# x as one row spread by TensorE, ScalarE's row sums as a register loop, GpSimd as a loop of eight units

## The chip, the cores and the metric

One Trainium2 chip, one core. The metric is the device time of one execution in microseconds (us); lower is better. A verdict of faster or slower needs a difference of 2%. An execution over 1.5% above the fastest of its kernel is called slow, a single one unknown, any other fast.

## The reference, cut to what matters

Two independent attention blocks, A and B, each decode one token for a batch of 2, with 32 heads, a cache of 8192 positions and a head width of 192. Each has its own x, caches and weights:

```python
q = (x @ wq)                                   # x: (2, 1, 640)
scores = einsum("bhqd,bhkd->bhqk", q, k_cache) * 192 ** -0.5
p = softmax(scores)
o = einsum("bhqk,bhkd->bhqd", p, v_cache)
out = o.reshape(2, 1, 32 * 192) @ wo           # then A and B side by side
```

Every K and V is read once: 2 blocks x 2 batches x 32 heads = 128 units, each with 3 MB of K and 3 MB of V. With the weights that is 836.77 MB from HBM, the chip's main memory.

## The kernel before

Each unit multiplies its K by the query, broadcast to all partitions. VectorE forms the products of all 64 rows and sums 48 of them by halving; the other 16 rows ScalarE sums with one activation each. GpSimd finds the maximum over partitions, ScalarE takes the exponential, TensorE multiplies by V. SyncE issues all loads; K and V have two buffers each.

```python
def sp_x(blk, b):                              # x, one batch: 640 elements to [128, 5]
    src = blocks[blk]["x"][b, 0, :].rearrange("(c j) -> j c", j=128)
    ...
            return eng.dma_start(xT[blk][b][:], src).then_inc(xsem[blk], 16)

def xbc_copy(blk, b):                          # spread over 128 columns, for TensorE's weights
    return lambda eng: eng.tensor_copy(xbc[blk][b][:], xT[blk][b][:].unsqueeze(2).broadcast_to([128, DC, 128]))

def act_acc(u, t):                             # ScalarE: the sum of one row
    return lambda eng: eng.activation(prodA[u % 2][:, t, :], prodA[u % 2][:, t, :], ACTF.Identity,
                                      accum_out=sc[u % 2][:, t:t + 1])
...
for t in range(na_of(u)):                      # 16 rows, written out
    w = [("d1a", u), key("d3", u - 2), key("exp", u - 2)] if t == 0 else []
    put(act_tab, u, 10 + t, act_acc(u, t), w, ("acc", u) if t == na_of(u) - 1 else None)
...
# SyncE's order at the start: x of A (2 loads), wq, K0 (2 parts), wq, x of B (2 loads), K1, V0, ...
# K(u) waits until VectorE has read K(u-2); V(u) waits until TensorE has read V(u-2)
...
S_sp.emit(eng)          # every instruction written out
S_pool.emit(eng)        # every instruction written out
S_dve.emit(eng, 8)      # steady middle as a hardware loop with a body of 8 units
S_act.emit(eng, 8)
S_pe.emit(eng, 4)
```

`emit(eng, period)` finds the longest stretch of the program that repeats after `period` units and puts it into a register loop, then searches what lies before and after it in the same way. What is left, as at the two ends and the seam of blocks A and B, stays written out.

Of the kernel before, what the change touches and what calls it, by code (L numbers as in the profile page):

```python
# [6 lines left out]
ACTF = mybir.ActivationFunctionType  # L7
AXL = mybir.AxisListType
BF16 = mybir.dt.bfloat16
# [93 lines left out]
def build_kernel(nc, blocks, out, cfg=None):  # L103
    cfg = dict(cfg or {})
    NBLK = len(blocks)
    B, Hn, Sk, Dh = blocks[0]["k"].shape
    D = blocks[0]["x"].shape[2]
    assert B == 2 and Dh == 192 and Sk % 256 == 0 and D % 128 == 0
    T = Sk // 128
    DC = D // 128  # L110
# [4 lines left out]
    scale = float(Dh) ** -0.5  # L115

    NA_MAIN = min(cfg.get("NA", 16), T - 2)
    LAG = cfg.get("LAG", 2)
    LATE = LAG - 1
    NPB = 4  # L120
# [14 lines left out]
    def na_of(u):  # L135
        return NA_MAIN

# [10 lines left out]
    with ExitStack() as es:  # L148
        sb = lambda name, shape, dt, align=32: es.enter_context(nc.sbuf_tensor(name, shape, dt, align_bytes=align))
# [10 lines left out]
        prodA = [sb(f"prodA{i}", [128, NA_MAX, Dh], BF16) for i in range(2)]  # L160
        prodD = sb("prodD", [128, ND_MAX, Dh], BF16)
        sc = [sb(f"sc{i}", [128, T], F32) for i in range(2)]
# [3 lines left out]
        pb = [sb(f"pb{i}", [128, T // 2, 33], BF16) for i in range(NPB)]  # L166
        rs = [sb(f"rs{i}", [128, 1], F32) for i in range(2)]
        qbc = [sb(f"qbc{i}", [128, 2, Dh], BF16) for i in range(4)]
        xT = [[sb(f"xT{k}_{b}", [128, DC], BF16) for b in range(B)] for k in range(NBLK)]
        xbc = [[sb(f"xbc{k}_{b}", [128, DC, 128], BF16) for b in range(B)] for k in range(NBLK)]  # L170
        o_sb = sb("o_sb", [33, 2, 2, Dh], F32)
        ones33 = sb("ones33", [33, 1], F32)
# [5 lines left out]
        actd = sb("actd", [128, 2], F32)  # L178
# [6 lines left out]
        reg = {}  # L185
# [16 lines left out]
        def key(name, *idx):  # L202
            for i in idx:
                if i < 0:
                    return None
            return (name,) + tuple(idx)
# [27 lines left out]
        reg[("wq0b",)] = (wq0sem, 16)  # L234
        WQSPLIT = HG >= 4
        for k in range(NBLK):
            reg[("x", k)] = (xsem[k], 16 * B)
            reg[("odone", k)] = (osem[k], 32)

        def dma(out_ap, in_ap, s):  # L240
            return lambda eng: eng.dma_start(out_ap, in_ap).then_inc(s, 16)  # L241

        def sp_x(blk, b):
            src = blocks[blk]["x"][b, 0, :].rearrange("(c j) -> j c", j=128)

            def fn(eng):
                with nc.allow_non_contiguous_dma(reason="tiny x transpose load"):
                    return eng.dma_start(xT[blk][b][:], src).then_inc(xsem[blk], 16)  # L248
            return fn

        def sp_wq(w, part=None):
            blk = (w * HG) // Hn
# [35 lines left out]
                return dma(v_tile(u)[:], src, vsem[u % NV])  # L288
            return dma(v_tile(u)[:, t0:t1, :], src[:, t0:t1, :], sm)

        def xbc_copy(blk, b):
            return lambda eng: eng.tensor_copy(xbc[blk][b][:], xT[blk][b][:].unsqueeze(2).broadcast_to([128, DC, 128]))

        def pool_ar(u):
            return lambda eng: eng.partition_all_reduce(mg[u % 2][:], mp[u % 2][:], 128, bass.bass_isa.ReduceOp.max)  # L295
# [30 lines left out]
            s0 = 64 * (g % 2)  # L326
            return lambda eng: eng.reciprocal(rcT[(g // 2) % 2][s0:s0 + 64, :], lall[g % 2][s0:s0 + 64, :])

        def act_acc(u, t):
            return lambda eng: eng.activation(prodA[u % 2][:, t, :], prodA[u % 2][:, t, :], ACTF.Identity,  # L330
                                              accum_out=sc[u % 2][:, t:t + 1])

        def act_nb(u):
            return lambda eng: eng.activation(nb[u % 2][:], mg[u % 2][:], ACTF.Identity, scale=-scale)  # L334
# [45 lines left out]
        def pe_p0(qg):  # L380
            pr, b = qg // 2, qg % 2
            g0 = 2 * pr
            blk = g0 // Hn
            w = g0 // HG
            npr = HG // 2

            def at(slot, off):
                def fn(eng):
                    for c in range(DC):
                        ins = eng.matmul(qps[:, 0:QW], xbc[blk][b][:, c, :],  # L390
                                         wqs[:, slot, c, off].rearrange("p a n -> p (a n)") if slot is not w % 2 else
                                         wqs[:, slot, c, off],
                                         start=(c == 0), stop=(c == DC - 1))
                    return ins
                return fn
            fn = at(w % 2, slice((pr % npr) * QW, (pr % npr + 1) * QW))
            fn.same = (blk, b)
            fn.turn = lambda it: at(bass.ds((it + pr) // npr % 2, 1), bass.ds((it + pr) % npr * QW, QW))
            return fn, [("wq", w) if w == 0 else None, ("wq0b",) if (w == 0 and WQSPLIT and pr % npr >= 1) else None,
                        ("xbc", blk), key("a0", qg - 1)]  # L400

        def pe_pv(u, j0, j1):
            b = u % B
# [58 lines left out]
        def put(tab, slot, order, fn, waits, sig):  # L462
            tab[slot].append((order, len(tab[slot]), fn, waits, sig))

        for u in range(NU):
            g = u // B
            put(dve_tab, u + 1, 0, dve_d3(u), [("acc", u), ("r", u), key("ar", u - 2)], ("d3", u))
            put(dve_tab, u, 2, dve_d1a(u), [("k", u), ("a0", qg_of(u)), key("acc", u - 2)], ("d1a", u))
            put(dve_tab, u, 3, dve_d1b(u), [("k", u), ("kb", u) if u in KSPLIT else None, ("a0", qg_of(u)),
                                            key("r", u - 1)], ("d1b", u))  # L470
            put(dve_tab, u, 4, dve_lvl(u, 96), [("d1b", u)], ("l1", u))
            put(dve_tab, u, 5, dve_lvl(u, 48), [("l1", u)], ("l2", u))
            put(dve_tab, u, 6, dve_lvl(u, 24), [("l2", u)], ("l3", u))
            put(dve_tab, u, 7, dve_r(u), [("l3", u), key("d3", u - 2), key("exp", u - 2)], ("r", u))
            put(pool_tab, u + 1, 0, pool_ar(u), [("d3", u), key("nb", u - 2)], ("ar", u))
            put(pool_tab, u + 1, 1, pool_ls(u), [("exp", u), key("f2", g - 2)], ("ls", u))
            put(act_tab, u + 1, 0, act_nb(u), [("ar", u), key("exp", u - 2)], ("nb", u))
            put(act_tab, u + 1, 1, act_exp(u), [("nb", u), ("acc", u), ("r", u), key("pv", u - NPB)], ("exp", u))
            for t in range(na_of(u)):
                w = [("d1a", u), key("d3", u - 2), key("exp", u - 2)] if t == 0 else []  # L480
                put(act_tab, u, 10 + t, act_acc(u, t), w, ("acc", u) if t == na_of(u) - 1 else None)
            pc = pieces(u)
            w0 = [("exp", u), key("f1", g - 2), ("init",)]
            if pc is None:
                put(pe_tab, u + LATE, 0, pe_pv(u, 0, T // 2), w0 + [("v", u)], ("pv", u))
            else:
                for i, (t0, t1, sm) in enumerate(pc):
                    put(pe_tab, u + LATE, 0.1 * i, pe_pv(u, t0 // 2, t1 // 2), (w0 if i == 0 else []) + [("vp", u, i)],
                        ("pv", u) if i == len(pc) - 1 else None)
# [59 lines left out]
                    S_sp.add(sp_v(u, t0, t1, sm), waits=w)  # L549

        UG = HG * B
        for b in range(B):
            S_sp.add(sp_x(0, b))
        S_sp.add(sp_wq(0, 0) if WQSPLIT else sp_wq(0))
        korder = []
        nv = 0
# [8 lines left out]
        for kind, u in korder:  # L565
            if kind == "k":
                if u in KSPLIT:
                    S_sp.add(sp_k(u, 0), waits=[key("d1b", u - NK)])
                    S_sp.add(sp_k(u, 1))
                else:  # L570
                    S_sp.add(sp_k(u), waits=[key("d1b", u - NK)])
                if u == 0:
                    if WQSPLIT:
                        S_sp.add(sp_wq(0, 1))
                    for blk in range(1, NBLK):
                        for b in range(B):
                            S_sp.add(sp_x(blk, b))
                w = u // UG
                if u % UG == (4 if UG >= 8 else 1):
                    S_sp.add(sp_wo(w), waits=[key("f5", (w - 1) * HG // 2)])  # L580
                if u % UG == (3 if UG >= 8 else 0) and w + 1 < NWG:
                    S_sp.add(sp_wq(w + 1), waits=[key("pq", w * HG)])
            else:
                add_v(u)
# [4 lines left out]
            S_pool.add((lambda i: (lambda eng: eng.memset(pb[i][:], 0.0)))(i))  # L589
        S_pool.add(lambda eng: eng.memset(oTz[:], 0.0))  # L590
        S_pool.add(lambda eng: eng.memset(oTzL[:], 0.0), sig=("init",))
        for blk in range(1, NBLK):
            for b in range(B):
                S_pool.add(xbc_copy(blk, b), waits=[("x", blk)], sig=("xbc", blk) if b == B - 1 else None)
        for b in range(B):
            S_dve.add(xbc_copy(0, b), waits=[("x", 0)], sig=("xbc", 0) if b == B - 1 else None)
        S_act.add(lambda eng: eng.memzero(actd[:, 0:1]), sig=("actd",))
        S_act.add(lambda eng: eng.activation(actd[:, 1:2], actd[:, 0:1], ACTF.Exp), waits=[("actd",)])

        for tab, S in ((dve_tab, S_dve), (act_tab, S_act), (pe_tab, S_pe), (pool_tab, S_pool)):  # L600
            for slot in range(NSLOT):
# [4 lines left out]
        with nc.Block() as block:  # L606
            @block.sync
            def _(eng):
                S_sp.emit(eng)

            @block.gpsimd
            def _(eng):
                S_pool.emit(eng)

            @block.vector
            def _(eng):
                S_dve.emit(eng, 8)

            @block.scalar
            def _(eng):  # L620
                S_act.emit(eng, 8)

            @block.tensor
            def _(eng):
                S_pe.emit(eng, 4)
# [49 lines left out]
```

## Time and profile before

| | before |
|---|---|
| time in us: first three runs, median | 1959.01 (1957.16 to 1959.31) |
| profiled execution | 1957.15, span 1955.3 |
| HBM read | 836.77 MB, 428 GB/s over the span |
| DMA busy | 9 tenths or more in each of 40 slices |
| VectorE, TensorE, ScalarE, GpSimd busy | 85%, 57%, 46%, 8% |

The page of the kernel before, cut to the span, the DMA packets, the two queues that fetch instructions (the engines' programs, piece by piece as they run), and two groups (busy us, mean ns of one, then the idle time before them):

```profile
span 1955.3 us, 18519 instructions
...
DMA packets 56618, 837.10 MB, mean 428 GB/s; under 512 B 7432, under 2 KB 18320, under 8 KB 24208
...
q8 instruction: 11, 0.18, 0.0%
q14 instruction: 15, 0.12, 0.0%
...
L330 ACT ACTIVATE prodA<-prodA 128x192 bf16<-128x192 bf16 x2048 | 709.3, 350 | 125.3 <-DVE prodA L308 124.8
...
L315 DVE TENSOR_REDUCE mp<-sc 128x1 f32<-128x64 f32 x128 | 28.2, 220 | 13.8 <-issue 4.9
```

The kernel is bound by the DMA engines. The maximum over scores (L315), which needs ScalarE's sums as well as VectorE's, waits 13.8 us in the whole run, so ScalarE isn't late. The instruction fetches stand at 0.0% of the engines' time.

SyncE's issues in the timeline of the kernel before (start, length, what):

```profile
0.72 0.98 SPq L248 DMA_DIRECT2D xT<-in_A_x_dram  x2
1.75 0.52 SPq L241 DMA_DIRECT2D wqs<-in_A_wq_dram  x1
2.31 1.00 SPq L241 DMA_DIRECT2D kb<-in_A_k_cache_dram  x2
3.35 0.43 SPq L241 DMA_DIRECT2D wqs<-in_A_wq_dram  x1
3.83 7.38 SPq L248 DMA_DIRECT2D xT<-in_B_x_dram  x2
...
11.25 0.54 SPq L241 DMA_DIRECT2D kb<-in_A_k_cache_dram  x1
11.83 2.26 SPq L241 DMA_DIRECT2D vb<-in_A_v_cache_dram  x1
```

The first large load goes out behind two x loads. Two more hold SyncE for 7.4 us ahead of K1.

### The profile page before, as it was taken

How to read it: one execution, taken by the hardware profiler on the slowest of the kernel's cores; microseconds unless marked ns; L12 is line 12 of the kernel's file. 1: busy time of each engine (PE TensorE's matmuls, PEld its weight loads, DVE VectorE, ACT ScalarE, POOL GpSimd, SP SyncE). 2: the span in 40 equal slices, each digit the busy share in tenths (PEclk: the TensorE clock that was granted, in tenths of full speed). 3: DMA queues.
4: the chain of work that ended last, by engine and by line, in shares of the span. 5: the costliest groups of instructions: out<-in, count | busy, mean ns of one | idle time of the engine just before them, and what ended most of it. 6: DMA issues, size and time to landing. Idle time of an engine off the chain costs nothing.

```text
span 1955.3 us, 18519 instructions
## 1 busy us (share of the span) xinstructions
PE 1110.9 (57%) x5004; PEld 588.5 (30%) x5004; DVE 1656.2 (85%) x962; ACT 903.2 (46%) x4743; POOL 165.8 (8%) x270
## 2 busy tenths in 40 slices
PE   3455655656556564565556655556555556655567
PEld 1222332323223232332223332233332333323234
DVE  7799888888988889887988889888798788888886
ACT  4445454444544445444454445444454454444543
POOL 4103000000000000000000000000000000000000
PEclk7777777777777777777777767777677777777778
DMA  9999999999999999999999999999999999999998
GB/s 385 430 433 428 433 431 432 433 430 432 431 432 432 431 434 430 432 433 429 432 430 433 431 430 433 431 431 434 429 433 430 432 433 432 431 429 435 432 433 338
DMA packets 56618, 837.10 MB, mean 428 GB/s; under 512 B 7432, under 2 KB 18320, under 8 KB 24208
## 3 DMA queue, kind: packets, MB, share of 16 engines
q1 hardware_dynamic: 56576, 836.79, 99.9%
q8 instruction: 11, 0.18, 0.0%
q14 instruction: 15, 0.12, 0.0%
q10 hardware_dynamic: 16, 0.01, 0.0%
HBM read 836.77 MB, written 0.01 MB: 428 GB/s over the span
## 4 chain that ended last, share of the span: by engine, by line
DMA 74%; PE 23%; DVE 2%; issue 0%; SPq 0%; ACT 0%; DVEq 0%
DMA vb<-in_B_v_cache_dram 37%; DMA vb<-in_A_v_cache_dram 33%; PE ops L408 23%; DMA kb<-in_A_k_cache_dram 4%; DVE prodD L312 2%; DVE prodD L319 1%; DVE prodA L308 0%; DVE sc L323 0%; SPq L241 0%; PE oTps L428 0%; PE outps L444 0%; SPq L248 0%; DVE mp L315 0%; ACT out_sb L372 0%; ACT o_sb L353 0%
## 5 line engine op out<-in xcount | busy, mean ns | idle before, releaser
L408 PE MATMUL ops<-vb,pb 128*33 128x384 bf16 x4064 | 944.9, 407 | 830.7 <-DMA vb<-in_A_v_cache_dram 443.1
L408 PEld LDWEIGHTS ops<-vb,pb 128*33 128x33 bf16 x4064 | 476.1, 120 | 1297.9 <-issue 578.2
L330 ACT ACTIVATE prodA<-prodA 128x192 bf16<-128x192 bf16 x2048 | 709.3, 350 | 125.3 <-DVE prodA L308 124.8
L312 DVE TENSOR_TENSOR prodD<-kb,qbc 128x9216 bf16<-128x9216 bf16 x128 | 633.7, 4951 | 3.7 <-DMA kb<-in_A_k_cache_dram 3.7
L319 DVE TENSOR_TENSOR prodD<-prodD 128x4608 bf16<-128x4608 bf16 (+2 forms) x384 | 599.0, 1560 | 13.3
L308 DVE TENSOR_TENSOR prodA<-kb,qbc 128x3072 bf16<-128x3072 bf16 x128 | 225.2, 1759 | 243.1 <-DMA kb<-in_B_k_cache_dram 127.6
L330 ACT ACTIVATION_READ_ACCUMULATOR prodA<-prodA 128x1 f32 x2048 | 387.9, 189 | 0.0
L334 ACT ACTIVATE nb<-mg 128x1 f32<-128x1 f32 x128 | 26.0, 203 | 725.8 <-POOL mg L295 725.8
L295 POOL PARTITION_ALL_REDUCE mg<-mp x128 | 53.7, 419 | 1652.6 <-DVE mp L315 1652.6
L323 DVE TENSOR_REDUCE sc<-prodD 128x48 f32<-128x1152 bf16 x128 | 173.2, 1353 | 4.4
L299 POOL PARTITION_ALL_REDUCE lall<-rs x128 | 101.3, 791 | 111.1 <-ACT pb L337 111.1
L344 ACT ACTIVATE o_sb<-ops 1x384 f32<-1x384 f32 x63 | 30.1, 478 | 125.7 <-PE oTps L417 112.5
L417 PE MATMUL oTps<-ones,o_sb 33*128 33x1 f32 x372 | 69.8, 311 | 1.4 <-ACT o_sb L345 1.4
L417 PEld LDWEIGHTS oTps<-ones,o_sb 33*128 33x128 f32 x372 | 67.2, 258 | 11.3 <-issue 7.9
L390 PE MATMUL qps<-wqs,xbc 128*128 (+1 forms) x320 | 65.1, 335 | 6.8 <-DMA wqs<-in_A_wq_dram 6.0
L337 ACT ACTIVATE pb<-sc,nb 128x64 bf16<-128x64 f32 x128 | 52.2, 408 | 13.0
L368 ACT ACTIVATE qbc<-qps 128x384 bf16<-128x384 f32 x64 | 31.4, 491 | 45.1 <-PE qps L390 45.0
L315 DVE TENSOR_REDUCE mp<-sc 128x1 f32<-128x64 f32 x128 | 28.2, 220 | 13.8 <-issue 4.9
L390 PEld LDWEIGHTS qps<-wqs,xbc 128*128 128x128 bf16 x320 | 26.4, 99 | 31.2 <-issue 10.5
L345 ACT ACTIVATE o_sb<-ops 1x384 f32<-1x384 f32 x63 | 30.4, 482 | 0.7
L444 PE MATMUL outps<-wos,oTz 128*4 (+1 forms) x186 | 30.3, 299 | 0.5 <-ACT oTz L362 0.5
L337 ACT ACTIVATION_READ_ACCUMULATOR pb<-sc,nb 128x1 f32 x128 | 23.9, 186 | 0.0
(27 smaller groups left out, 68.4 us busy)
## 6 DMA issues: line engine op xcount, KB each, us to landing
vb<-in_A_v_cache_dram SPq DMA_DIRECT2D x64, 3072.0 KB, 22.2
kb<-in_B_k_cache_dram SPq DMA_DIRECT2D x64, 3072.0 KB, 22.4
kb<-in_A_k_cache_dram SPq DMA_DIRECT2D x63, 3072.0 KB, 22.4
vb<-in_B_v_cache_dram SPq DMA_DIRECT2D x61, 3072.0 KB, 22.1
wos<-in_A_wo_dram SPq DMA_DIRECT2D x8, 960.0 KB, 26.8
wqs<-in_B_wq_dram SPq DMA_DIRECT2D x8, 960.0 KB, 24.5
wos<-in_B_wo_dram SPq DMA_DIRECT2D x8, 960.0 KB, 26.8
wqs<-in_A_wq_dram SPq DMA_DIRECT2D x7, 960.0 KB, 24.5
```

The source lines that it names most:

```text
L295: return lambda eng: eng.partition_all_reduce(mg[u % 2][:], mp[u % 2][:], 128, bass.bass_isa.ReduceOp.max)
L299: return lambda eng: eng.partition_all_reduce(lall[g % 2][:, b:b + 1], rs[u % 2][:], 128, bass.bass_isa.ReduceOp.add)
L308: return lambda eng: eng.tensor_tensor(prodA[u % 2][:, 0:na, :], kb[u % NK][:, 0:na, :], qb_bc(u, na), ALU.mult)
L312: return lambda eng: eng.tensor_tensor(prodD[:, 0:T - na, :], kb[u % NK][:, na:T, :], qb_bc(u, T - na), ALU.mult)
L319: return lambda eng: eng.tensor_tensor(prodD[:, 0:nd, 0:w], prodD[:, 0:nd, 0:w], prodD[:, 0:nd, w:2 * w], ALU.add)
L323: return lambda eng: eng.tensor_reduce(sc[u % 2][:, na:T], prodD[:, 0:T - na, 0:24], AXL.X, ALU.add)
L330: return lambda eng: eng.activation(prodA[u % 2][:, t, :], prodA[u % 2][:, t, :], ACTF.Identity, accum_out=sc[u % 2][:, t:t + 1])
L337: return lambda eng: eng.activation(pb[u % NPB][:, :, ::32], sc[u % 2][:].rearrange("p (j a) -> p j a", a=2), ACTF.Exp, bias=nb[u % 2][:], ...
L368: return lambda eng: eng.activation(qbc[qg % 4][:], qps[:, 0:QW].rearrange("p (a d) -> p a d", a=2), ACTF.Identity)
L390: ins = eng.matmul(qps[:, 0:QW], xbc[blk][b][:, c, :], wqs[:, slot, c, off].rearrange("p a n -> p (a n)") if slot is not w % 2 else wqs[:, ...
L408: ins = eng.matmul(ops[(u // B) % 2][0:33, b, 0:QW], pb[u % NPB][:, j, :], vv[:, j, :], start=(j == 0), stop=(j == T // 2 - 1))
L417: ins = eng.matmul(oTps[:, 2 * i + b:2 * i + b + 1], o_sb[:, b, :, :].rearrange("p s (r i) -> p i (s r)", i=3)[:, i, :], ones33[:], start= ...
```

## The change

Its intent: take 2560 two-byte packets and their issue time off SyncE at the start; write ScalarE's 16 row sums as a register loop, five turns of three and one left over; give GpSimd's stream the loop that the others have. Cut to its core:

```diff
+        xrow = [sb(f"xrow{k}", [1, B, DC, 128], BF16) for k in range(NBLK)]
+        one1 = sb("one1", [1, 128], BF16)
...
-        def sp_x(blk, b):                      # 4 loads on SyncE, element by element
+        def ld_x(blk):                         # 2 loads on ScalarE's queue, x as one row
+            src = blocks[blk]["x"].rearrange("b o (c j) -> o b c j", j=128)
+            return dma(xrow[blk][:], src, xsem[blk])
...
-        def xbc_copy(blk, b): ...
+        def pe_x(blk, b):                      # TensorE spreads the row: row chunk x ones
+            def fn(eng):
+                for c in range(DC):
+                    ins = eng.matmul(xps(b)[:, c, :], xrow[blk][0:1, b, c, :], one1[:], start=True, stop=True)
+                return ins
+            return fn
+        # then PSUM to xbc: VectorE for A's batch 0, ScalarE for the other three
...
-        def act_acc(u, t): ...
+        def act_acc(u):
+            na = na_of(u); nl = (na - 1) // ROWS * ROWS          # ROWS = 3
+            def fn(eng):
+                ...
+                with eng.Fori(0, nl - ROWS + 1, ROWS) as i:
+                    for k in range(ROWS):
+                        one(pa[:, bass.ds(i + k, 1), :], s[:, bass.ds(i + k, 1)])
+                for t in range(nl, na):
+                    ins = one(pa[:, t, :], s[:, t:t + 1])
+                return ins
...
-                S_pool.emit(eng)
+                S_pool.emit(eng, 8)
```

More of the change, by code (lines that the diff above doesn't have):

```diff
@@ L117, in build_kernel @@
     NA_MAIN = min(cfg.get("NA", 16), T - 2)
+    ROWS = 3
     LAG = cfg.get("LAG", 2)
@@ L168, in build_kernel @@
         qbc = [sb(f"qbc{i}", [128, 2, Dh], BF16) for i in range(4)]
-        xT = [[sb(f"xT{k}_{b}", [128, DC], BF16) for b in range(B)] for k in range(NBLK)]
+        xrow = [sb(f"xrow{k}", [1, B, DC, 128], BF16) for k in range(NBLK)]
+        one1 = sb("one1", [1, 128], BF16)
         xbc = [[sb(f"xbc{k}_{b}", [128, DC, 128], BF16) for b in range(B)] for k in range(NBLK)]
@@ L236, in build_kernel @@
         for k in range(NBLK):
-            reg[("x", k)] = (xsem[k], 16 * B)
+            reg[("x", k)] = (xsem[k], 16)
             reg[("odone", k)] = (osem[k], 32)
@@ L241, in dma @@
             return lambda eng: eng.dma_start(out_ap, in_ap).then_inc(s, 16)
-        def sp_x(blk, b):
-            src = blocks[blk]["x"][b, 0, :].rearrange("(c j) -> j c", j=128)
-            def fn(eng):
-                with nc.allow_non_contiguous_dma(reason="tiny x transpose load"):
-                    return eng.dma_start(xT[blk][b][:], src).then_inc(xsem[blk], 16)
-            return fn
+        def ld_x(blk):
+            src = blocks[blk]["x"].rearrange("b o (c j) -> o b c j", j=128)
+            return dma(xrow[blk][:], src, xsem[blk])
         def sp_wq(w, part=None):
@@ L289, in sp_v, with xps, act_x, dve_x @@
             return dma(v_tile(u)[:, t0:t1, :], src[:, t0:t1, :], sm)
-        def xbc_copy(blk, b):
-            return lambda eng: eng.tensor_copy(xbc[blk][b][:], xT[blk][b][:].unsqueeze(2).broadcast_to([128, DC, 128]))
+        def xps(b):
+            return ops[b][:].rearrange("p a n -> p (a n)")[:, 0:D].rearrange("p (c m) -> p c m", m=128)
+        def pe_x(blk, b):
[4 more added lines that the diff above has]
+            return fn
+        def act_x(blk, b):
+            return lambda eng: eng.activation(xbc[blk][b][:], xps(b), ACTF.Identity)
+        def dve_x(blk, b):
+            return lambda eng: eng.tensor_copy(xbc[blk][b][:], xps(b))
         def pool_ar(u):
@@ L327, in dve_f2, with one @@
             return lambda eng: eng.reciprocal(rcT[(g // 2) % 2][s0:s0 + 64, :], lall[g % 2][s0:s0 + 64, :])
-        def act_acc(u, t):
-            return lambda eng: eng.activation(prodA[u % 2][:, t, :], prodA[u % 2][:, t, :], ACTF.Identity,
-                                              accum_out=sc[u % 2][:, t:t + 1])
+        def act_acc(u):
+            na = na_of(u)
+            nl = (na - 1) // ROWS * ROWS
+            def fn(eng):
+                pa, s = prodA[u % 2], sc[u % 2]
+                def one(row, col):
+                    return eng.activation(row, row, ACTF.Identity, accum_out=col)
+                with eng.Fori(0, nl - ROWS + 1, ROWS) as i:
[4 more added lines that the diff above has]
+                return ins
+            return fn
         def act_nb(u):
@@ L399, in pe_p0 @@
             return fn, [("wq", w) if w == 0 else None, ("wq0b",) if (w == 0 and WQSPLIT and pr % npr >= 1) else None,
-                        ("xbc", blk), key("a0", qg - 1)]
+                        ("xbc", blk, b), key("a0", qg - 1)]
         def pe_pv(u, j0, j1):
@@ L478, in build_kernel @@
             put(act_tab, u + 1, 1, act_exp(u), [("nb", u), ("acc", u), ("r", u), key("pv", u - NPB)], ("exp", u))
-            for t in range(na_of(u)):
-                w = [("d1a", u), key("d3", u - 2), key("exp", u - 2)] if t == 0 else []
-                put(act_tab, u, 10 + t, act_acc(u, t), w, ("acc", u) if t == na_of(u) - 1 else None)
+            put(act_tab, u, 10, act_acc(u), [("d1a", u), key("d3", u - 2), key("exp", u - 2)], ("acc", u))
             pc = pieces(u)
@@ L551, in build_kernel @@
         UG = HG * B
-        for b in range(B):
-            S_sp.add(sp_x(0, b))
         S_sp.add(sp_wq(0, 0) if WQSPLIT else sp_wq(0))
@@ L574, in build_kernel @@
                         S_sp.add(sp_wq(0, 1))
-                    for blk in range(1, NBLK):
-                        for b in range(B):
-                            S_sp.add(sp_x(blk, b))
                 w = u // UG
@@ L591, in build_kernel @@
         S_pool.add(lambda eng: eng.memset(oTzL[:], 0.0), sig=("init",))
+        S_dve.add(lambda eng: eng.memset(one1[:], 1.0), sig=("one1",))
+        for blk in range(NBLK):
+            S_act.add(ld_x(blk))
+        for b in range(B):
+            S_pe.add(pe_x(0, b), waits=[("x", 0), ("one1",)], sig=("xp", 0, b))
+        S_dve.add(dve_x(0, 0), waits=[("xp", 0, 0)], sig=("xbc", 0, 0))
+        S_act.add(lambda eng: eng.memzero(actd[:, 0:1]), sig=("actd",))
+        S_act.add(lambda eng: eng.activation(actd[:, 1:2], actd[:, 0:1], ACTF.Exp), waits=[("actd",)])
+        S_act.add(act_x(0, 1), waits=[("xp", 0, 1)], sig=("xbc", 0, 1))
         for blk in range(1, NBLK):
             for b in range(B):
-                S_pool.add(xbc_copy(blk, b), waits=[("x", blk)], sig=("xbc", blk) if b == B - 1 else None)
-        for b in range(B):
-            S_dve.add(xbc_copy(0, b), waits=[("x", 0)], sig=("xbc", 0) if b == B - 1 else None)
-        S_act.add(lambda eng: eng.memzero(actd[:, 0:1]), sig=("actd",))
-        S_act.add(lambda eng: eng.activation(actd[:, 1:2], actd[:, 0:1], ACTF.Exp), waits=[("actd",)])
+                put(pe_tab, 0, -0.5, pe_x(blk, b), [("x", blk), ("xbc", 0, b)], ("xp", blk, b))
+                put(act_tab, 0, -0.5, act_x(blk, b), [("xp", blk, b)], ("xbc", blk, b))
         for tab, S in ((dve_tab, S_dve), (act_tab, S_act), (pe_tab, S_pe), (pool_tab, S_pool)):
```

## The prediction

> **What bounds the kernel: the DMA engines.** The page has their busy share at 9 tenths or more in all 40 slices; the span is 1955.3 us for 836.77 MB from HBM. The table of stages shows 430 to 433 GB/s in every stretch from 100 to 1920 us. 836.77 MB at 432 GB/s is 1937 us, so at most 18 us can go unless bytes or rate change; the change touches neither. The chain of waits agrees: 74% DMA. ScalarE is 46% busy, GpSimd 8%, VectorE 85%. A unit takes about 14.5 us; K lands 22 us after its issue though it moves in about 7, so some 15 us of transfers are always queued ahead.
>
> **x (start only).** In the timeline SyncE issues two x loads (0.72 to 1.70 us), then wq, K0, wq, then two x loads of block B, which hold it 7.38 us (3.83 to 11.21); K1 is issued at 11.25. The Trainium skill, "DMA: Bandwidth & Descriptors", Rules for kernel authors, says a non-contiguous last dim becomes one descriptor per element; the trace agrees: 2560 packets of 2 bytes. The change has ScalarE issue two row loads, and TensorE spread them.
> - wq and K0 go out 1.03 us earlier.
> - K1 and V0 go out right behind, near 3 us. In the table of stages the rate falls to 337, 323 and 271 GB/s in single microseconds between 12 and 16. The shortfall against 432 GB/s summed from 4 to 24 us is about 1.4 us (an estimate); most should go.
> - The new chain to the first query (row lands near 3 us, five matmuls, a PSUM copy of about 0.8 us) should meet wq, which lands near 5 us. It isn't on the path that frees K0: that waits for K0's second half, landing at 13.88 now, near 12.5 then.
> - GpSimd loses 6.1 us of copies, ScalarE gains three of about 0.75 us. Both idle there.
>
> Worth: 1.03 plus about 1.2: 2.2 us off the span.
>
> **ScalarE's rows as a register loop.** The work stays 16 pairs, started 0.346 us apart, 5.6 us a unit. Added per unit: five branches and register addresses. The loops already there show the price in the raw records: ScalarE's closing branch 0.045 to 0.050 us, register operations 0.035 to 0.050, hidden behind the activations. If some show, 0 to 2 us a unit. Slack: near 1000 us the first product ends at 1003.3, so the row sums end near 1008.9; the maximum over scores also waits for VectorE's own reduction, ending at 1014.3. About 5 us spare, and the DMA's queue behind that. Worth 0.
>
> **GpSimd as a loop.** Waits on register values, a fraction of a microsecond; its reductions take 0.42 and 0.79 us per 14.5. Worth 0, as is the smaller program: instruction fetches are 0.3 MB of 837.
>
> **Prediction:** 1959.0 - 2.2 = 1956.8 us; 8 in 10: 1954.0 to 1959.3. Faster by over 2%: 0.01; within 2%: 0.97; slower by over 2%: 0.02.
>
> **What would show each step.**
> - Timeline: first wq issue near 0.7, K1 near 3 us, no dip of the rate at 12 to 16; packets under 512 B down by about 2500.
> - Row sums still start about 0.35 us apart; the maximum over scores still waits almost nowhere (13.8 us idle in total now).
> - The middle still at 430 to 433 GB/s; the end, 8.6 us after the last V piece (1946.7), unchanged.
>
> **What would make it wrong.** Register addressing or re-fetching at the inner branch costs over 5 us a unit, so that the maximum waits for ScalarE and VectorE (85% busy) falls behind the DMA: each extra microsecond then costs up to 128, and the time passes 2000. Or a shift of the DMA's rate by 0.1% (2 us, the spread of the three runs) drowns the gain.

## More of the kernel before

The end of the kernel before in the table of stages (stretch, its length, busy us of each engine, granted clock, DMA share, GB/s):

```profile
1942.00:1944.00 2.00, 2.00 (x18) 1.51 (x17) 0.00 (x0) 0.64 (x2) 0.00 (x0) 1.00 0.99 410
1944.00:1946.00 2.00, 2.00 (x15) 1.19 (x13) 0.00 (x0) 0.00 (x0) 0.00 (x0) 1.00 0.69 280
1946.00:1948.00 2.00, 1.76 (x11) 0.78 (x9) 0.00 (x0) 0.00 (x0) 0.00 (x0) 1.00 0.18 71
```

The rate doesn't stop at once. It falls to two thirds and then to a sixth: some of the 16 engines have finished and others have not.

## The result, and the profile after

| | before | after |
|---|---|---|
| time in us: median of four runs | 1958.09 (1956.98 to 1959.31) | 1953.56 (1953.47 to 1953.77) |
| ratio, with its 95% interval | | 0.9977 (0.996 to 0.9994) |
| profiled execution | 1957.15 | 1953.77 |

Ratios are the mean time of one kernel's fast runs over that of the other's fast runs of the same rounds, so not quite the ratio of the medians quoted. The class came out as foreseen (no change of 2%), but the gain is 4.5 us where 2.2 were forecast, and 1953.56 lies just under the stated range. The changed kernel's runs also agree within 0.3 us, where those of before spread over 2.3. All outputs are right.

The page after, the lines that answer to those of before:

```profile
span 1952.0 us, 22103 instructions
...
DMA packets 53995, 837.07 MB, mean 429 GB/s; under 512 B 4810, under 2 KB 15698, under 8 KB 21588
...
q8 instruction: 11, 0.18, 0.0%
q14 instruction: 12, 0.10, 0.0%
...
L348 ACT ACTIVATE prodA<-prodA (+1 forms) x2048 | 710.9, 354 | 139.2 <-DVE prodA L319 139.1
...
L326 DVE TENSOR_REDUCE mp<-sc 128x1 f32<-128x64 f32 x128 | 28.2, 220 | 13.9 <-issue 5.0
```

2622 short packets are gone. The row sums cost the same, and the maximum over scores still waits for nobody: on ScalarE itself the register loop costs nothing. Queue q14 fetched three packets fewer, 12 instead of 15.

The issues at the start, in the timeline after:

```profile
0.71 0.55 ACTq L243 DMA_DIRECT2D xrow<-in_A_x_dram  x1
...
0.72 0.43 SPq L243 DMA_DIRECT2D wqs<-in_A_wq_dram  x1
...
1.21 0.98 SPq L243 DMA_DIRECT2D kb<-in_A_k_cache_dram  x2
1.29 0.23 ACTq L243 DMA_DIRECT2D xrow<-in_B_x_dram  x1
...
2.71 0.67 SPq L243 DMA_DIRECT2D kb<-in_A_k_cache_dram  x1
...
3.42 0.44 SPq L243 DMA_DIRECT2D vb<-in_A_v_cache_dram  x1
```

wq goes out at 0.72 us and K1 at 2.71, as foreseen. The end after, in the table of stages:

```profile
1940.00:1942.00 2.00, 2.00 (x16) 1.34 (x16) 0.00 (x0) 0.00 (x0) 0.00 (x0) 1.00 0.97 399
1942.00:1944.00 2.00, 1.76 (x12) 0.85 (x10) 0.00 (x0) 0.00 (x0) 0.00 (x0) 1.00 0.52 210
1944.00:1946.00 2.00, 2.00 (x15) 1.30 (x14) 0.00 (x0) 0.27 (x1) 0.00 (x0) 1.00 0.06 23
```

The end has the same shape. The stretches of the two tables don't line up with the two ends, so how far the last engine trails can't be read off them; that takes the raw records.

### Two numbers from the raw records

The Trainium skill, "DMA: Bandwidth & Descriptors", Why a DMA increments its semaphore by 16 and not by 1, says that each engine that takes part posts one increment once its own data has landed. The trace agrees: each K or V load shows 16 increments, each with its time. From them, and from the records of the packets, two numbers can be worked out for every run:

- **start**: the time at which the first 15 MB have arrived. The core is well into the steady state by then.
- **lag**: on the last V load, the last engine's increment minus the mean of the 16.

```
profiled run                  time us   start    lag   time - start - lag
before                        1957.15   40.78   2.47   1913.90
after                         1953.77   38.14   1.68   1913.95
```

What is left over is the same to 0.05 us. So the two traces differ by 3.38 us in two places: 2.64 us in the first 40, and 0.79 us because the slowest of the 16 DMA engines trails the others less at the end. The middle is unchanged. The remaining 1.2 us of the measured 4.5 are the distance of the two profiled executions from their medians: 0.9 us in the kernel before, which section 4 takes up, and 0.2 in the changed one.

### The profile page after: what moved, and what is told of

Same layout as the page of the kernel before. It is cut to its first block, busy times and chain, and to the rows that moved or that the text cites. A ratio compares the mean times of both kernels' runs of the same rounds, so it can differ in the third digit from the quotient of the medians.

```text
span 1952.0 us, 22103 instructions
## 1 busy us (share of the span) xinstructions
PE 1119.9 (57%) x5024; PEld 592.0 (30%) x5024; DVE 1654.8 (85%) x962; ACT 905.9 (46%) x4746; POOL 162.0 (8%) x268
## 4 chain that ended last, share of the span: by engine, by line
DMA 73%; PE 23%; DVE 2%; issue 0%; SPq 0%; ACT 0%; DVEq 0%
DMA vb<-in_B_v_cache_dram 37%; DMA vb<-in_A_v_cache_dram 33%; PE ops L432 23%; DMA kb<-in_A_k_cache_dram 4%; DVE prodD L323 2%; DVE prodD L330 0%; DVE prodA L319 0%; DVE sc L334 0%; SPq L243 0%; PE oTps L452 0%; PE outps L468 0%; DVE mp L326 0%; ACT out_sb L396 0%; ACT o_sb L377 0%; ACT oTzL L386 0%
## 5 line engine op out<-in xcount | busy, mean ns | idle before, releaser
L348 ACT ACTIVATE prodA<-prodA (+1 forms) x2048 | 710.9, 354 | 139.2 <-DVE prodA L319 139.1
L348 ACT ACTIVATION_READ_ACCUMULATOR prodA<-prodA (+1 forms) x2048 | 396.3, 193 | 0.0
L326 DVE TENSOR_REDUCE mp<-sc 128x1 f32<-128x64 f32 x128 | 28.2, 220 | 13.9 <-issue 5.0
```

The costliest lines, as they stand in the source:

```text
L348: return eng.activation(row, row, ACTF.Identity, accum_out=col)
```

## The experiments

Two theories stood at the outset. *Start only*: the x part gives everything, the loops nothing, and scatter explains the rest. *Start plus lag*: the loops change which instruction fetches are made, each fetch holds up one DMA engine, and the kernel ends with the slowest engine.

### 1. The parts alone

Four kernels on one chip, five rounds each. The x part alone (row sums and GpSimd as before):

```diff
-            put(act_tab, u, 10, act_acc(u), ...)
+            for t in range(na_of(u)): put(act_tab, u, 10 + t, act_acc(u, t), ...)
-                S_pool.emit(eng, 8)
+                S_pool.emit(eng)
```

> Kernel before with the x part of the change alone. Theory S (start only): the whole gain is the x part, so the mean is 4.2 to 4.8 us under that of before, and the profile shows bytes 2.5 us ahead from the first 30 us on. Theory L (start plus lag): bytes 2.5 us ahead at the start, and in the end the last DMA engine still lags the mean of the 16 by about 2.5 us as before (1.7 in the changed kernel), so the mean gain is 2.5 to 3.8 us. On the scatter: if the two-byte packets cause it, the five runs agree within 0.5 us; if not, they scatter by 2 us as before.

Both loops, x as before (the kernel before with the new `act_acc` and `S_pool.emit(eng, 8)`):

> Kernel before with both loops, x as before. Theory S: within 0.4 us of before. Theory L: 0.5 to 1.5 us under before, with the lag of the last DMA engine near 1.7 us at the end, and no gain in the first 100 us. Runs scatter by 2 us if the two-byte packets cause it.

ScalarE's loop alone (the kernel before with the new `act_acc`):

> Kernel before with ScalarE's inner loop alone. Theory S: within 0.4 us of before. Theory L: anything from -1 to +1 us, and the difference equals the difference of the last DMA engine's lag at the end. Row sums start 0.346 us apart on average as before, up to 0.36.

GpSimd's loop alone:

```diff
-                S_pool.emit(eng)
+                S_pool.emit(eng, 8)
```

> Kernel before with GpSimd's period loop alone. Theory S: within 0.4 us of before. Theory L: GpSimd's instruction fetches (3 packets of 8 KB fewer) vanish and the lag of the last DMA engine changes by 0 to -0.9 us, the time with it.

Measured (the kernel before in the same rounds: 1957.09 to 1959.46, nine runs, median 1958.80):

```
                     five runs, us                            ratio (95%)
x part alone         1955.67 1955.53 1955.62 1956.05 1955.64  0.9986 (0.9972 to 0.9999)
both loops           1956.57 1956.48 1956.21 1960.50 1956.04  0.9994 (0.998 to 1.0007)
ScalarE's loop       1956.26 1956.20 1956.08 1960.62 1962.72  1.0002 (0.9988 to 1.0015)
GpSimd's loop        1958.87 1958.98 1957.15 1957.05 1959.33  0.9998 (0.9984 to 1.0011)

profiled run         time us   start    lag   time - start - lag
x part alone         1955.67   38.18   3.49   1914.00
both loops           1956.57   40.95   1.66   1913.95
ScalarE's loop       1956.26   40.71   1.66   1913.89
GpSimd's loop        1958.87   42.45   2.43   1913.99
```

The ratios alone would call both loops and ScalarE's loop nothing, because single slow executions lie in them. The two columns separate what the ratios can't. The x part alone has the whole start (2.60 us), but it gained less than the change, because its lag is 3.49. ScalarE's loop alone takes the lag from 2.47 to 1.66 and leaves the start; GpSimd's loop alone does neither (its start of 42.45 is that of the slow stretch in section 4). So *start only* falls: the x part was not worth 4.2 us. *Start plus lag* stands. Its range for the x part held (2.7 us between the means, 1958.40 and 1955.70), though it expected a lag of 2.5. What it expected of GpSimd's loop didn't come: the page of that run has 16 fetches on q14, not 3 fewer than 15. Each row of the table is one execution, but the lag repeats: 2.47, 2.47 and 2.44 in the three traces in which every engine but SyncE has the program of before (sections 3 and 4), 1.68, 1.58 and 1.39 in the changed kernel and its two near copies of section 3.

Fetches go with it, but not one for one. The pages of the x part alone and of ScalarE's loop alone, instruction queues:

```profile
q8 instruction: 11, 0.18, 0.0%
q14 instruction: 17, 0.14, 0.0%
```

```profile
q8 instruction: 11, 0.18, 0.0%
q14 instruction: 12, 0.10, 0.0%
```

In the raw records of before, 8 KB fetches at 1841.6, 1888.1 and 1896.5 us are each followed by a rise of the last engine's lag, from 1.85 to 2.96 us in all (2.63 one load later). In the x part alone fetches at 1793.2 and 1840.1 us are followed by a rise of 0.6 us each, and two at 1893.0 and 1894.9 by 0.9 (0.6 one load later); hence its 3.49. ScalarE's loop has only two of q14's fetches after 1790 and before 1900, at 1824.0 and 1896.4; neither raises its lag, which stays below 2. So it matters where a fetch falls. The records don't name the engine; that these two fell on engines with time to spare is a guess.

### 2. What a fetch costs: ScalarE's program written out

If fetches on one engine are what matters, many more of them should show it. The changed kernel, with ScalarE's rows and units all written out:

```diff
-            put(act_tab, u, 10, act_acc(u), ...)
+            for t in range(na_of(u)): put(act_tab, u, 10 + t, act_acc(u, t), ...)
...
-                S_act.emit(eng, 8)
+                S_act.emit(eng)
```

> The changed kernel with ScalarE's whole program written out (no loop of any kind on it, the same activations in the same order). Nothing waits more, and only about 0.3 MB of instruction fetches are added. If fetches cost their share of the bytes, the time is within 0.7 us of the changed kernel. If each 8 KB fetch holds up one of the 16 DMA engines by about 0.85 us, some 35 to 40 added fetches make the time 2 to 6 us longer than the changed kernel (1955.5 to 1959.5), with the bytes at 1900 us 1.5 to 2.5 us later and a larger lag of the last engine, and the start unchanged.

It took 1973.78 us (1973.18 to 1974.38; ratio to before 1.0078, 1.0064 to 1.0092), 20 us more than the changed kernel and beyond even the range of the fetch theory. A rival would be that ScalarE itself falls behind; but the maximum over scores (L325) waits only 13.2 us in the whole run (13.8 in the kernel before). Its page:

```profile
span 1972.5 us, 18381 instructions
...
DMA packets 54028, 837.34 MB, mean 425 GB/s; under 512 B 4810, under 2 KB 15698, under 8 KB 21588
...
q14 instruction: 45, 0.37, 0.0%
q8 instruction: 11, 0.18, 0.0%
...
L325 DVE TENSOR_REDUCE mp<-sc 128x1 f32<-128x64 f32 x128 | 28.2, 220 | 13.2 <-issue 4.3
```

0.27 MB more in 837 cost 1%. By its share of the bytes it would have cost 0.6 us. The records show why: the lag grows steadily, 1.4 us at 200 us, 4.5 at 500, 7.6 at 800, 9.7 at 1000, and stays at 10 to 11. It grows in steps: of the 17 fetches on q14 between 200 and 1000 us, 16 are each followed by a rise of 0.56 to 0.65 us; the one at 493.3, which the changed kernel makes too (489.7), is not. The increments don't name the engines, but the second-latest stays within 1.5 us of the mean, so it is one engine that trails, and these fetches nearly all seem to fall on it. Up to about 10 us the queued transfers hide it: up to 500 MB the bytes are within 0.4 us of the changed kernel's. From there on the other 15 engines wait for that one: at 800 MB the bytes are 10.4 us behind, and in the end the time left over (time - start - lag) is 12.5 us higher. Together 20.6 us for 33 more packets of 8 KB: 0.62 us each, twice the 0.31 us that such a packet takes in the records. Why twice, no run shows.

The end of this run in the table of stages:

```profile
1950.00:1956.00 6.00, 4.87 (x28) 2.24 (x26) 5.86 (x5) 1.95 (x8) 0.00 (x0) 1.00 0.84 347
1956.00:1960.00 4.00, 3.21 (x20) 1.61 (x19) 0.80 (x4) 0.75 (x4) 0.73 (x2) 1.00 0.08 31
1960.00:1964.00 4.00, 3.81 (x29) 2.50 (x29) 0.00 (x0) 0.54 (x2) 0.00 (x0) 1.00 0.06 26
```

For eight microseconds 26 to 31 GB/s move, which is a sixteenth of 432 GB/s (27): one engine finishing alone.

### 3. What the start gained: the packets or the order

My prediction credited the start to issue times: wq 1.03 us earlier and K1 out early. First, block B's element-wise loads moved behind K1 and V0, all else as before:

```diff
-                    for blk in range(1, NBLK):           # x of B, ahead of K1
-                        for b in range(B): S_sp.add(sp_x(blk, b))
...
                 add_v(u)
+                if u == 0:                               # x of B, behind V0
+                    for blk in range(1, NBLK):
+                        for b in range(B): S_sp.add(sp_x(blk, b))
```

> Kernel before with block B's two x loads moved on SyncE behind K1 and V0; block A's two stay first. The first wq still goes out at 1.75 us, K1 near 3.9 us. Bytes at 40 us are 1.2 to 1.6 us ahead of before: the share of K1's late issue. The other 1.0 us of the start stays lost. Scatter: as in the run with x on ScalarE's queue, whichever it is.

All five runs lay at 1956.99 to 1957.23 (ratio 0.9994, 0.998 to 1.0009). K1 left early in the timeline:

```profile
3.92 0.61 SPq L241 DMA_DIRECT2D kb<-in_A_k_cache_dram  x1
...
5.05 6.93 SPq L248 DMA_DIRECT2D xT<-in_B_x_dram  x2
```

But start is 40.78 us, exactly that of the profile of before. In the packet records the first 10 MB were complete 0.8 us earlier than before, and the first 12 MB no earlier: the moved x packets, which start between 28 and 30 us (14 and 16 before), had taken the lead back. So K1's late issue cost nothing net, and my 1.2 us for it is refuted. The records of before agree: from 8 to 40 us there are never fewer than 16 packets in flight, so the DMA engines weren't short of work at the dip.

Next, the element-wise loads on ScalarE's queue instead:

```diff
-        for b in range(B): S_sp.add(sp_x(0, b))          # and those of B, likewise
+        for blk in range(NBLK):
+            for b in range(B): S_act.add(sp_x(blk, b))
```

> Kernel before, its four element-wise x loads issued by ScalarE instead of SyncE, nothing else changed. If the start's gain is SyncE's issue time (wq 1.03 us earlier, K1 near 3 us instead of 11.25), bytes from 40 us on are 2.2 to 2.6 us ahead as in the changed kernel, in its undisturbed executions. If the 2560 two-byte packets themselves cost part of it, the lead is 1.0 to 1.8 us. The scatter: if the two-byte packets cause the slow stretch at 20 to 34 us (24 KB packets of 1.05 us instead of 0.91), some of the five runs are 2 us or more above the fastest; if K1 queueing behind them on one ring causes it, all five agree within 0.6 us.

It missed both expectations: 1969.30 us, 0.56% slower than before. SyncE was as free as in the changed kernel, yet start was only 0.66 us ahead, and then the run lost 13 us more. The timeline shows where:

```profile
1.87 8.82 ACTq L248 DMA_DIRECT2D xT<-in_B_x_dram  x2
...
14.69 1.54 DVE L292 COPY xbc<-xT 128x640 bf16<-128x640 bf16 x2 [14.69 <-DMA xT<-in_A_x_dram]
```

```profile
53.47 1.39 POOL L292 COPY xbc<-xT 128x640 bf16<-128x640 bf16 x2 [48.22 <-DMA xT<-in_B_x_dram]
54.99 0.35 POOL L295 PARTITION_ALL_REDUCE mg<-mp  x1
```

A's x lands at 14.69 us instead of 4.14, B's at 53.47, and GpSimd's first maximum stands behind B's copy, so the first exponential waits until 55 us and the queue runs dry: next to nothing moves from 54 to 64 us. The Trainium skill, "DMA: Bandwidth & Descriptors", Queues, rings and completion order, says that each engine goes round its queue rows packet by packet. The trace fits: on a row of its own each tiny packet takes turns with 18 to 24 KB packets of K and V. B's 1280 packets, 80 to an engine, came in over some 40 us. Most came in bursts; between 30 and 50 us, with the queue full, 255 came, one per engine in 1.25 us, where a 24 KB packet takes 0.91. The form of the load and the choice of queue go together: a row of few packets can afford the second queue.

Then the rows, but on SyncE in the old places:

```diff
-        for blk in range(NBLK): S_act.add(ld_x(blk))
+        S_sp.add(ld_x(0))                                # ahead of the first wq
...
+                    S_sp.add(ld_x(1))                    # behind the second wq, ahead of K1
```

> The changed kernel with the two row loads issued by SyncE in the old places (A's before wq, B's after the second wq), so that only the form of the loads and what spreads them differ from before, not their queue. If the two-byte packets were the larger part of the loss, bytes at 40 us are still 1.8 to 2.3 us ahead of before (the rest, 0.3 to 0.7 us, is wq's issue behind A's row), and the time is 0.3 to 0.7 us over the changed kernel. If the order of issue was the larger part, the lead falls below 1.5 us. No run shows the slow stretch at 20 to 34 us: all five within 0.5 us.

1953.95 us (1953.83 to 1954.09, six runs), start 38.55. So of the 2.64 us, the rows in place of elements give 2.23 and the second queue 0.41. Its timeline:

```profile
0.72 0.33 SPq L243 DMA_DIRECT2D xrow<-in_A_x_dram  x1
1.11 0.41 SPq L243 DMA_DIRECT2D wqs<-in_A_wq_dram  x1
```

wq leaves 0.64 us before it did in the kernel before (1.75) and 0.39 after it does in the changed one. Last, the packets by themselves. The changed kernel with the four old loads added in the middle of the run, where nobody reads them and the queue is full:

```diff
             else:
                 add_v(u)
+                if u in (20, 26, 32, 38):
+                    S_sp.add(sp_xd((u - 20) // 6))       # old element-wise load into a spare tile
```

> The changed kernel with the four old element-wise x loads (2560 two-byte packets, about 3.7 us of SyncE each) added in the middle of the run, after V of units 20, 26, 32 and 38, into buffers that nobody reads. The queue holds some 15 us of transfers there, so SyncE being held costs nothing. If the packets themselves cost the DMA engines time, the bytes fall 1.2 to 2.2 us behind the changed kernel between 250 and 600 us and stay there, and the time is 1954.8 to 1955.8. If only SyncE's late issues counted at the start, the time stays within 0.3 us of 1953.6.

1954.98 us (1954.68 to 1955.24, six runs), 1.4 us over the changed kernel. Start and lag are as in the changed kernel (37.98 and 1.58), and the time left over is 1915.29 instead of 1913.95. So 2560 two-byte packets cost 1.3 us even where SyncE's issue time is free (it was held 0.44 us by each load there, not the 3.7 expected). The records give each such packet 9 ns: 160 to an engine make 1.4 us. At the start, then, 2.23 us for the form is an estimate of about 1.3 for the packets, 0.64 for wq's earlier issue, and 0.3 that no run separates.

### 4. Why the executions of before scatter

> The kernel before once more, unchanged, for its scatter. If the executions near 1959 differ from those near 1957 by the slow stretch alone that the run with GpSimd's loop showed (24 KB packets of 1.05 us instead of 0.91 between 20 and 34 us), then this execution is either at 1957.0 to 1957.4 with 430 GB/s there, or at 1958.5 to 1959.5 with 370 to 380 GB/s there and bytes 1.5 to 2 us later from 40 us on, and everything after that, the last engine's lag too, is as in the first profile.

This execution took 1959.42 us (a single one, so its state is unknown; its clock, 0.735, is that of the others). Its time left over is 1913.91 and its lag 2.47, both as in the first profile, and its start is 43.05 instead of 40.78. The kernel before, first profile and this one, in the table of stages:

```profile
22.00:24.00 2.00, 0.00 (x0) 0.00 (x0) 1.97 (x2) 0.00 (x0) 0.40 (x1) 0.50 0.97 418
24.00:26.00 2.00, 0.00 (x0) 0.00 (x0) 1.86 (x3) 0.00 (x0) 0.00 (x0) 0.50 1.03 442
26.00:28.00 2.00, 0.00 (x0) 0.00 (x0) 2.00 (x3) 0.00 (x0) 1.78 (x1) 0.50 1.00 430
```

```profile
22.00:24.00 2.00, 0.00 (x0) 0.00 (x0) 1.97 (x2) 0.00 (x0) 0.31 (x1) 1.00 1.05 393
24.00:26.00 2.00, 0.00 (x0) 0.00 (x0) 1.86 (x4) 0.00 (x0) 0.00 (x0) 1.00 1.02 381
26.00:28.00 2.00, 0.00 (x0) 0.00 (x0) 2.00 (x3) 0.00 (x0) 1.78 (x1) 1.00 1.02 381
```

The DMA engines are just as busy but move 356 to 393 GB/s from 16 to 34 us. The profiled execution of GpSimd's loop alone has the same stretch: there 24 KB packets take 1.05 us instead of 0.91. It is K1 and V0, the two loads behind x of B; from 34 us on all is as usual. The granted clock differs in these lines too (0.50 and 1.00), but it isn't the cause: the run with x of B behind V0 has 1.00 there and 406 to 467 GB/s.

In the rounds of the other experiments, 12 of 29 executions of before lie under 1957.5 and 17 over 1958.4. None of the row kernels did this: within the changed kernel, the x part alone, the kernels of sections 2 and 5, the rows on SyncE and the added packets, runs agree within 0.2 to 1.2 us. Nor did the five runs with B's element-wise loads moved behind V0 (within 0.24) or the five with x on ScalarE's queue (within 0.91). So here the slow stretch came only with the element-wise loads ahead of K1 on SyncE's queue. What makes it come in some executions and not in others no run shows. A few executions of before and of the loops alone went higher still (1960.5 to 1990.8, the last slow; 1969.17 in this section); none of those was profiled.

### 5. A smaller program for TensorE

If fetches matter, the 16 KB fetches of q8 should be worth something as well. They stood beside the written-out parts of TensorE's program, so that program was shrunk: the 32 PV matmuls of a unit as a register loop, the first and last written out.

```diff
-                for j in range(j0, j1):
-                    ins = eng.matmul(ops[(u // B) % 2][0:33, b, 0:QW], pb[u % NPB][:, j, :], vv[:, j, :],
-                                     start=(j == 0), stop=(j == T // 2 - 1))
+                one(eng, 0, True, False)
+                with eng.Fori(1, T // 2 - PVR, PVR) as i:        # PVR = 10, then 5
+                    for k in range(PVR): one(eng, i + k, False, False)
+                return one(eng, T // 2 - 1, False, True)
```

> The changed kernel with the 32 PV matmuls of a unit as a register loop on TensorE (first and last written out, 3 turns of 10), so that TensorE's program and its 16 KB fetches shrink (11 now). If fetches set the last engine's lag, the time falls by 0.3 to 1.2 us (1952.4 to 1953.3) and the queue of TensorE's fetches shows 3 to 6 packets. If they do not matter, it is within 0.2 us, or slower if TensorE's loop delays the release of V buffers by more than the queue covers (TensorE then over 75% busy).

1953.56 us (1953.43 to 1953.59), q8 down from 11 to 9 and not to 3 to 6. No gain: the lag fell to 1.07 us near 1890 us, where the changed kernel has 1.89, but after a fetch of q14 at 1892.9 us it rose to 1.57, and after one of q8 at 1938.7 from 1.34 to 1.75; it ended at 1.67. (The next expectation puts both fetches after 1900; of the two on q8 there, the one at 1904.0 raised nothing.)

> The changed kernel with the PV matmuls as a register loop with six turns of 5 instead of three turns of 10, to shrink TensorE's program further. The run with turns of 10 cut the 16 KB fetches from 11 to 9 and the last engine's lag at 1890 us from 1.9 to 1.1 us, but two fetches after 1900 us brought it back to 1.67. If fewer fetches move the late ones out, the time falls by 0.2 to 0.6 us under the changed kernel; if the late ones stay, it is within 0.2 us.

1953.37 us (1953.17 to 1953.42, six runs; ratio to before 0.9970, 0.9949 to 0.9991), q8 at 7, lag 1.76. That is 0.2 us under the changed kernel, which was timed in another call; 0.58 us under the rows on SyncE, which ran in the same one. It is the lowest time, but 0.01% is not a gain to keep a more complicated kernel for, with TensorE's busy share at 69% instead of 57%. Its lag rises from 1.17 to 2.00 after a fetch of q14 at 1893.2 us, which neither loop removes. The 0.4 us between the profiled executions of this kernel and the changed one stand neither in start (38.14) nor in lag but in the time left over (1913.48); no run separates their cause.

## Why the prediction was wrong

**The bound** was right: DMA, with a middle that none of the parts changed. The time left over, 1913.89 to 1914.00 in before, after, the four parts and two of the start's variants, says so.

**The start** was forecast at 2.2 us and measured at 2.64. The sum was nearly right, by luck; its terms were not. "wq and K0 go out 1.03 us earlier" held. "K1 and V0 go out right behind, near 3 us", worth 1.2 us with the rate's dip at 12 to 16, failed: with K1 out at 3.92 us the start didn't move. The dip was not a queue waiting for SyncE: 16 packets were in flight throughout. In its place stand the 2560 packets themselves, 1.3 us by the run that added them in the middle. I had counted those packets and not costed them.

**ScalarE's loop** on its own engine was right: row sums still 0.35 us apart, and the maximum idle for 13.9 us against 13.8.

**"Worth 0, as is the smaller program: instruction fetches are 0.3 MB of 837"** was the step of the mechanism that failed. It took a share of the bytes as a share of the time. A fetch can put one of the 16 engines behind (0.56 to 0.65 us each in section 2), every load is complete only when its last engine is, and so the engine that is furthest behind sets the end. On top of before, ScalarE's loop was worth 0.8 us that way and GpSimd's 0. On top of the x part the two together were worth 1.8 (a lag of 3.49 against 1.68); there no run separates the two loops. **"The end ... unchanged"** failed with it: the chain after the last landing is unchanged, but the landing itself comes 0.79 us less behind the mean.

**The baseline** was mis-sized too, and this is the largest part of the miss. I subtracted from 1959.0, the median of three runs, but the trace I had costed was an execution of 1957.15. The two differ by the slow stretch at 16 to 34 us, as far as the two profiled executions near 1959 tell. I named the spread of the runs only as noise that might drown the gain, although the change takes its condition away. Of the 3.2 us between 1956.8 and 1953.56, 1.9 come from this, 0.8 from the lag, 0.4 from the start, and 0.2 from the spread of the changed kernel's own runs.

## What to carry to other kernels

When one resource is busy from end to end, look at it engine by engine, not on average: a load is complete when its last DMA engine is, so what falls on a single engine can cost its time there in full (here up to 0.62 us for an instruction fetch of 8 KB), however small its share of the bytes. Before costing a change of a few microseconds, ask which of the executions the profile shows and whether the change touches the cause of the spread. An element-wise load can cost three times: in issue (wq left 0.64 us later), in DMA time wherever it stands (1.3 us for 2560 packets), and in latency once it shares the engines with large packets of another queue (x at 53.47 us).

## What the Trainium skill lacked or had wrong

- "Runtime: NRT & Kernel Launch", Instruction fetch mechanics, calls the cost of fetching the next block "mostly hidden". From ScalarE, which fetched, it was hidden here; from the DMA engines, which bind this kernel, it wasn't: 33 more 8 KB fetches cost 20.6 us, 0.62 us each against a packet time of 0.31, and it is one of the 16 engines that they put behind.
- No page says that instruction fetches can put one DMA engine further and further behind through a whole run, or that queued loads hide this only up to a depth (about 10 us here). "DMA: Bandwidth & Descriptors" has the 16 increments from which it can be measured: 1.4 to 3.5 us at the end of most runs, 9.8 with ScalarE written out.
- "DMA: Bandwidth & Descriptors", Rules for kernel authors, warns of element-wise loads but gives no cost in a full queue (the page's one time per packet, under Measured, is of loads issued from GpSimd): 1.3 us for 2560 two-byte packets, 9 ns each in the records. Its advice that a second issuing engine only saves issue time holds for rows (0.41 us); with element-wise loads the second queue also made x land at 53.47 us instead of about 16.
- No page has the slow stretch: 24 KB packets of 1.05 us instead of 0.91 for two loads behind element-wise ones, in some executions only.
